# Reordering the start of a diffusion transformer block: silu first, matvecs ahead of transposes, two engines sharing the PSUM copies, a third transpose buffer

## The chip, the cores and the metric

The kernel runs on one core of one Trainium2 chip. The metric is the device time of one execution in microseconds (us), lower is better. The engines are named as the profile names them: PE (TensorE, matmuls), PEld (its weight loads), DVE (VectorE), ACT (ScalarE), POOL (GpSimd), SP (the engine that issues most DMAs here). The span that the profile gives is shorter than the device time: by 1.7 to 1.8 us in the executions of the kernel before.

All ratios are the mean time of one kernel's fast runs over that of the other's fast runs of the same rounds, so they are not quite the ratio of the medians that stand beside them.

## The reference

One block of a diffusion transformer, with B = 2, N = 256 (so 512 rows), D = 1152, two heads and an MLP of width 4608, in bf16:

```python
mod = (silu(c) @ w_mod).reshape(B, 6, 1, D)
shift_a, scale_a, gate_a, shift_m, scale_m, gate_m = [mod[:, i] for i in range(6)]
h = layernorm(x) * (1 + scale_a) + shift_a
q, k, v = split(h @ wqkv)
a = softmax(q @ k.T * Dh ** -0.5) @ v @ wo
x = x + gate_a * a
h2 = layernorm(x) * (1 + scale_m) + shift_m
return x + gate_m * (gelu(h2 @ w_fc1, approximate=True) @ w_fc2)
```

## The kernel before

The part that matters is the head: everything before the first matmul of q and k ("qk"). It needs two things. One is LayerNorm 1 of x, transposed (`lnT`). The other is the modulation: silu(c), transposed (`sT`), times the first six 384-column chunks of `w_mod` (54 small matmuls, called matvecs here). A chunk of weights is 128 x 9 x 384 bf16, 864 KB, in rows of 768 bytes. Each chunk's result is copied from PSUM, turned by three 128x2 matmuls into `modT`, and then `lnT` is multiplied and shifted into `hT`, which the qk matmuls read.

```python
ps_tr = ctx.enter_context(tc.tile_pool(name="ps_tr", bufs=2, space=PSUM))   # transposes
# silu(c): one exp on ACT, three small operations on DVE
nc.scalar.activation(out=c_e, in_=cT_ps, func=ACT.Exp, scale=-1.0)
nc.vector.tensor_scalar(...); nc.vector.reciprocal(...)
nc.vector.tensor_tensor(out=sT[:, :, 0:B], ...)
# ... in mod_mm_multi: 9 matvecs per chunk, then
    nc.vector.tensor_copy(out=m_sb, in_=ps[:, 0:CW])          # always DVE
# LayerNorm 1: statistics and normalisation of all four tiles on DVE
for t in range(TT):
    layernorm_tile(x_sb[:, t, :], ln, False)
for k in range(KD):                                            # 36 transposes
    for t in range(TT):
        nc.tensor.transpose(out=pt[:, t, :], in_=ln1[t][:, k*P:(k+1)*P], identity=ident)
    # copy to lnT, alternately by DVE and ACT
for g in range(NC3):                                           # three pairs of chunks
    m0 = mod_mm(g); m1 = mod_mm(NC3 + g)
    mod_fin_T(m0, g, 0, False); mod_fin_T(m1, NC3 + g, 1, True)
    # six modulations into hT, dealt out to DVE, ACT and POOL
# ... (cut) then qk_chunk(0, split=True): its weights in three column thirds, rows of 256 bytes
```

The source order is a priority for the scheduler, not the order on the engines. Each engine runs its own queue in order.

## Time and profile before

| Quantity | Before |
|---|---|
| Device time, median of 4 runs (lowest, highest) | 265.78 us (265.41, 266.69) |
| The execution that was profiled | 266.69 us, span 264.9 us |
| PE busy | 242.8 us, 92% of the span |
| First matvec; first qk matmul; second group of 9 qk matmuls | 16.43; 26.36; 28.62 us |
| Sixth chunk of `w_mod` landed; its matvecs start | 23.17; 24.38 us |

First, lines of the profile's page for the kernel before: busy time by engine, then busy tenths in 40 equal slices of 6.6 us each, and the granted clock of the array.

```profile
span 264.9 us, 3724 instructions
PE 242.8 (92%) x1556; PEld 135.4 (51%) x1567; DVE 79.7 (30%) x227; ACT 65.0 (25%) x138; POOL 16.8 (6%) x29
PE   0068999999999999998999999999999999999994
PEclk9999999999999999999999999999999999999999
```

PE is full from the fifth slice on, except for a dip at LayerNorm 2. So, apart from the tail in the last slice, time can only be won in the first four slices and in that dip. The clock row says full speed everywhere.

The timeline of PE in the kernel before: start, duration, line, operation, how many, and the idle time ahead with what ended it.

```profile
16.11 0.40 PE L259 MATMUL tr_ps<-ident,ln 128*128 128x128 bf16 x2 [1.26 <-DVE ln L222]
16.43 1.78 PE L135 MATMUL mod_ps<-wchunk,sT 128*32 128x384 bf16 x14
...
19.84 1.03 PE L259 MATMUL tr_ps<-ident,ln 128*128 128x128 bf16 x8
...
24.38 0.66 PE L135 MATMUL mod_ps<-wchunk,sT 128*32 128x384 bf16 x9
25.23 0.23 PE L158 MATMUL modT_ps<-sel4T,m_sb 128*128 128x2 bf16 x3 [0.20 <-DVE m_sb L147]
26.29 0.21 PE L158 MATMUL modT_ps<-sel4T,m_sb 128*128 128x2 bf16 x3 [0.83 <-DVE modT L163]
```

Fourteen matvecs take 1.78 us at 16.43 (127 ns each), nine take 0.66 us at 24.38 (73 ns each): the array is slow at first. PE runs the sixth chunk's matvecs at 24.38, 1.2 us after their weights landed, because it is late with the work ahead of them.

The chain of waits behind it in the kernel before, start and length in us:

```profile
24.22 0.42 DVE lnT L262
...
24.71 0.06 DVE m_sb L147
...
25.70 0.47 DVE m_sb L147
26.16 0.08 DVE modT L163
...
26.29 0.21 PE modT_ps L158 x3
26.50 2.07 PE qk_ps L308 x9
28.57 0.05 issue
28.62 1.46 PE qk_ps L308 x6
```

After the matvecs, the copies wait on DVE for their turn, and the qk matmuls wait for those.

Last, windows of the kernel before: from:to, length, then busy time of each engine (instructions), granted clock, DMA share, GB/s.

```profile
16.40:21.40 5.00, 5.00 (x42) 2.03 (x41) 2.62 (x8) 1.07 (x2) 0.55 (x1) 1.00 1.10 326
21.40:26.30 4.90, 3.83 (x60) 2.32 (x60) 4.53 (x15) 3.24 (x7) 2.24 (x4) 1.00 1.26 222
26.40:44.00 17.60, 17.49 (x82) 7.75 (x82) 3.53 (x7) 3.44 (x6) 1.27 (x2) 1.00 1.09 329
```

Once the qk matmuls run, PE leaves 0.1 us of 17.6 unused, so a head that ends earlier by some amount shortens the kernel by about that amount.

### The profile page before, as it was taken

What the parts mean: (1) busy time and instruction counts of PE and PEld (TensorE: products, weight loads), DVE (VectorE), ACT (ScalarE), POOL (GpSimd) and SP (SyncE); (2) the same over time, 40 slices, a digit from 0 to 9 for tenths busy, and PEclk for the clock granted to TensorE, in tenths of its full rate; (3) what the DMA queues carried; (4) which work ended last, traced back from release to release, by engine and by line L of the source; (5) the groups of instructions that cost most, each with busy time, mean ns of one, the idle gap of its engine ahead of it and who ended that gap; (6) DMA issues with size and microseconds to landing.
All of it is one profiled execution on the core that took longest, in us unless ns stands there. A gap on an engine that the chain in (4) does not pass through costs nothing.

```text
span 264.9 us, 3724 instructions
## 1 busy us (share of the span) xinstructions
PE 242.8 (92%) x1556; PEld 135.4 (51%) x1567; DVE 79.7 (30%) x227; ACT 65.0 (25%) x138; POOL 16.8 (6%) x29
## 2 busy tenths in 40 slices
PE   0068999999999999998999999999999999999994
PEld 0025444455565666567844444444466656666562
DVE  0877313445453746882100000000011111122111
ACT  2005210223312532687532332323300000000000
POOL 2113100022102000100000000000000000000000
PEclk9999999999999999999999999999999999999999
DMA  6999999999999998057265555544440193000000
GB/s 211 356 326 246 335 327 326 327 327 326 326 327 326 326 327 265 1 160 243 57 212 139 153 177 181 156 134 136 135 132 30 26 325 97 17 15 15 27 20 15
DMA packets 67755, 50.37 MB, mean 190 GB/s; under 512 B 4635, under 2 KB 67227, under 8 KB 67739
## 3 DMA queue, kind: packets, MB, share of 16 engines
q1 hardware_dynamic: 67136, 48.96, 63.0%
q10 hardware_dynamic: 603, 1.18, 1.2%
q8 instruction: 12, 0.20, 0.3%
q14 instruction: 4, 0.03, 0.0%
HBM read 48.96 MB, written 1.18 MB: 189 GB/s over the span
## 4 chain that ended last, share of the span: by engine, by line
PE 85%; DVE 5%; issue 3%; DMA 3%; ACT 2%; POOL 1%; ACTq 0%; POOLq 0%
PE f_ps L476 27%; PE f_ps L465 22%; PE qk_ps L308 13%; PE v_ps L322 7%; PE wo_ps L414 4%; PE mod_ps L135 4%; DMA x_sb<-in_x_dram 3%; PE f1h_ps L458 2%; PE o_ps L364 2%; PE s_ps L336 2%; DVE ln_stats L211 1%; PE tr_ps L259 1%; ACT ln L435 1%; PE gate_ps L169 1%; PE tr_ps L229 1%
## 5 line engine op out<-in xcount | busy, mean ns | idle before, releaser
L476 PE MATMUL f_ps<-wchunk,gT 128*128 128x384 bf16 x432 | 70.4, 326 | 0.0
L465 PE MATMUL f_ps<-h2T,wchunk 128*128 128x512 bf16 x264 | 58.1, 379 | 0.3
L476 PEld LDWEIGHTS <-gT 128*128 128x128 bf16 x432 | 42.3, 98 | 28.0
L484 DVE TENSOR_TENSOR f_tmp<-f_ps,gate_bc 128x384 f32<-128x384 f32 x12 | 6.7, 558 | 120.1 <-PE f_ps L476 120.1
L465 PEld LDWEIGHTS <-wchunk 128*128 128x128 bf16 x270 | 26.4, 98 | 31.6
L308 PE MATMUL qk_ps<-hT,wchunk 128*128 128x512 bf16 x157 | 35.5, 379 | 0.3
L466 ACT ACTIVATE gT<-f_ps 128x512 bf16<-128x512 f32 x30 | 17.9, 597 | 40.6 <-PE f_ps L465 39.2
L308 PEld LDWEIGHTS <-wchunk 128*128 128x128 bf16 x162 | 15.7, 98 | 18.7 <-issue 0.5
L414 PE MATMUL wo_ps<-wchunk,aT 128*128 128x384 bf16 x108 | 18.7, 326 | 0.0
L322 PE MATMUL v_ps<-wchunk,hT 128*128 128x384 bf16 x108 | 18.0, 326 | 0.0
L259 PE MATMUL tr_ps<-ident,ln 128*128 128x128 bf16 x36 | 4.3, 258 | 11.9 <-DVE ln L222 11.9
L322 PEld LDWEIGHTS <-hT 128*128 128x128 bf16 x108 | 10.6, 98 | 6.7
L414 PEld LDWEIGHTS <-aT 128*128 128x128 bf16 x108 | 10.3, 98 | 6.0
L458 PE MATMUL f1h_ps<-h2T,wchunk 128*128 128x256 bf16 x108 | 13.1, 272 | 0.0
L135 PE MATMUL mod_ps<-wchunk,sT 128*32 128x384 bf16 x162 | 11.7, 360 | 0.0
L458 PEld LDWEIGHTS <-wchunk 128*128 128x128 bf16 x108 | 10.3, 98 | 1.4 <-issue 0.2
L347 POOL TENSOR_SCALAR pn<-p_sb,rinv 128x256 bf16<-128x256 bf16 x8 | 7.3, 924 | 46.1 <-DVE rinv L345 46.1
L147 DVE CAST m_sb<-mod_ps 128x384 bf16<-128x384 f32 x18 | 9.4, 551 | 2.7 <-PE mod_ps L135 2.5
L259 PEld LDWEIGHTS <-ln 128*128 128x128 bf16 x36 | 2.4, 110 | 14.7 <-DVE ln L222 13.1
L211 DVE BATCH_NORM_STATS2 ln_stats<-x_sb 128x6 f32<-128x384 bf16 x12 | 6.0, 536 | 6.3 <-DMA x_sb<-in_x_dram 6.3
L422 ACT ACTIVATE sq_junk<-x 128x384 bf16<-128x384 f32 x12 | 6.2, 515 | 5.9 <-DVE x L418 4.3
L417 DVE TENSOR_TENSOR wo_tmp<-wo_ps,gate_bc 128x384 f32<-128x384 f32 x12 | 6.7, 555 | 2.2 <-PE wo_ps L414 2.2
(79 smaller groups left out, 155.6 us busy)
## 6 DMA issues: line engine op xcount, KB each, us to landing
wchunk<-in_w_fc_dram SPq DMA_DIRECT2D x24, 864.0 KB, 5.4
wchunk<-in_w_mod_dram SPq DMA_DIRECT2D x18, 864.0 KB, 10.2
wchunk<-in_wqkv_dram SPq DMA_DIRECT2D x8, 864.0 KB, 10.1
wchunk<-in_wo_dram SPq DMA_DIRECT2D x3, 864.0 KB, 10.1
x_sb<-in_x_dram ACTq DMA_DIRECT2D x4, 288.0 KB, 7.3
out_dram<-o_sb SPq DMA_DIRECT2D x12, 96.0 KB, 1.6
wchunk<-in_wqkv_dram SPq DMA_DIRECT2D x3, 288.0 KB, 7.6
c<-in_c_dram ACTq DMA_DIRECT2D x1, 4.5 KB
```

The costliest lines, as they stand in the source:

```text
L135: nc.tensor.matmul(ps[32 * g : 32 * (g + 1), 0:CW], lhsT=sT[:, k, :], rhs=wt[:, k, :], start=(g not in gs[:k]), stop=(g not in gs[k + 1 :] ...
L147: nc.vector.tensor_copy(out=m_sb, in_=ps[:, 0:CW])
L211: nc.vector.bn_stats(out=stats[:, i, :], in_=src[:, i * CW : (i + 1) * CW])
L259: nc.tensor.transpose(out=pt[:, t, :], in_=ln1[t][:, k * P : (k + 1) * P], identity=ident)
L308: nc.tensor.matmul(ps, lhsT=wt[:, k, i * P : (i + 1) * P], rhs=hT[:, k, :], start=(k == 0), stop=(k == KD - 1))
L322: nc.tensor.matmul(ps[:, 0:CW], lhsT=hT[:, k, t * P : (t + 1) * P], rhs=wt[:, k, :], start=(k == 0), stop=(k == KD - 1))
L347: nc.gpsimd.tensor_scalar(out=pn, in0=p_sb, scalar1=rinv[:, 0:1], scalar2=None, op0=ALU.mult)
L414: nc.tensor.matmul(ps[:, 0:CW], lhsT=aT[:, k, t * P : (t + 1) * P], rhs=wo_t[c3][:, k, :], start=(k == 0), stop=(k == KD - 1))
L458: nc.tensor.matmul(ps[:, 0:N], lhsT=wt[:, k, i * P : (i + 1) * P], rhs=h2T[:, k, b * N : (b + 1) * N], start=(k == 0), stop=(k == KD - 1))
L465: nc.tensor.matmul(ps, lhsT=wt[:, k, i * P : (i + 1) * P], rhs=h2T[:, k, :], start=(k == 0), stop=(k == KD - 1))
L466: nc.scalar.activation(out=gT[:, f, :], in_=ps, func=ACT.Gelu_apprx_tanh)
L476: nc.tensor.matmul(ps[:, 0:CW], lhsT=gT[:, kf, t * P : (t + 1) * P], rhs=wts[kf // KD][:, kf % KD, :], start=(kf == 0), stop=(kf == KF - 1),)
```

## The change

The intent is to let qk start earlier and to speed up the transposes in LayerNorm 2:

- silu(c) goes ahead of the LayerNorm statistics on DVE, and tiles 2 and 3 take their statistics on ACT;
- matvecs of the first chunks go ahead of the transposes on PE;
- the copies of the modulation alternate between DVE and ACT;
- four dummy matmuls stand in a wait for the last chunks;
- the transposes get three PSUM buffers in place of two.

The diff, cut to its core:

```diff
-    ps_tr = ctx.enter_context(tc.tile_pool(name="ps_tr", bufs=2, ...))
+    ps_tr = ctx.enter_context(tc.tile_pool(name="ps_tr", bufs=3, ...))
...
+    def warm(n, after):
+        wp = ps_tr.tile([P, 512], FP32, name="warm_ps", tag="tr")
+        for _ in range(n):
+            w = nc.tensor.matmul(wp, lhsT=ident, rhs=x_sb[:, 0, 0:512], start=True, stop=True)
+            order_after(w, after, "keep PE busy")
...
-            nc.vector.tensor_copy(out=m_sb, in_=ps[:, 0:CW])
+            if mod_evac_i[0] % 2 == 0:
+                cp = nc.vector.tensor_copy(out=m_sb, in_=ps[:, 0:CW])
+            else:
+                cp = nc.scalar.copy(out=m_sb, in_=ps[:, 0:CW])
...
+    def layernorm_tile_act(src, dst):
+        nc.scalar.activation(out=dst, in_=src, func=ACT.Identity, accum_out=s12[:, 0:1])
+        nc.scalar.activation(out=dst, in_=src, func=ACT.Square, accum_out=s12[:, 1:2])
+        ...
-    for g in range(NC3):
-        m0 = mod_mm(g)
-        m1 = mod_mm(NC3 + g)
-        ...
+    for t in (2, 0, 3, 1):
+        ln1_tile(t)
+    m_of[0] = mod_mm(0)
+    m_of[3] = mod_mm(3)
+    m_of[1] = mod_mm(1)
+    ln1_transposes(2, after=last_mod_mm[0])
+    ln1_transposes(0)
+    m_of[4] = mod_mm(4)
+    ln1_transposes(3, after=last_mod_mm[0])
+    ln1_transposes(1)
+    fin_pair(0)
+    modulate_group(0)
+    fin_pair(1)
+    m_of[2] = mod_mm(2)
+    first_after[0] = warm(4, last_mod_mm[0])
+    m_of[5] = mod_mm(5)
+    fin2 = mod_fin_T(m_of[2], 2, 0, False)
+    modulate_group(1, last_copy[0], fin2)
+    mod_fin_T(m_of[5], 5, 1, True)
+    modulate_group(2)
```

## The prediction

> **What bounds the kernel now.** TensorE. The engine table gives PE 242.8 of 264.9 us, and the slices show PE nearly full from the fifth slice to the end. In the windows view PE is busy 17.5 of 17.6 us (26.4 to 44) and 55.6 of 56 (44 to 100). So this change can only pay where PE still waits: before the first qk matmul at 26.36, and while LayerNorm 2 is transposed (123.9 to 128.3: PE busy 3.6 of 4.4 us).
>
> **The head now.** In the timeline the modulation matvecs start at 16.43, because silu(c) waits on VectorE behind the LN1 statistics (ready 16.13). They and 36 transposes keep PE full from 16.4 to 21.4, slowly: 14 matvecs took 1.78 us (127 ns each) at 16.4, 18 took 0.99 us (55 ns) at 44. The Trainium skill, "TensorE: Matmul & The Clock Gate", Part 1, says that an idle array runs at half clock until it has been busy for about 3.4 us; these spacings agree, though the page's clock row shows full clock throughout. The sixth matvec chunk runs at 24.38 to 25.04, although (issue plus time to landing) it landed at 12.9 + 10.3 = 23.2. A chain follows: PSUM copies on VectorE (the second ends 26.16), 128x2 matmuls, modT, modulations to 28.14. The ninth qk matmul waits for that; the second qk group starts at 28.62.
>
> **What the change does.** silu(c) comes before most LN1 work (tiles 2 and 3 take their statistics on ScalarE): matvecs should start near 14.4. Matvecs go ahead of transposes, evacuations alternate between VectorE and ScalarE, four dummy matmuls fill a wait, transposes get a third PSUM buffer. It adds about 1 us of PE dummies where PE would wait for the DMA, and about 5 us of ScalarE, idle there now.
>
> **On the critical path.** PE is no longer late for the sixth chunk, but cannot pass its landing, 23.2, nor the first third of the qk weights, 15.6 + 8.9 = 24.5; DMA moves 326 GB/s without a gap from 7 us on, and its order is not changed. From 23.2: matvecs 0.8, copy on ScalarE 0.5, matmuls and modT 0.5; but ScalarE then still has four modulations (1.1 us a pair), ending near 26.6. First qk matmul 24.7, second group 26.9: gain 1.7 us. It can hardly exceed 2: the second qk chunk lands only at 30.7, and PE will want it at 30.8.
>
> Third PSUM buffer: VectorE copies take 0.41, ScalarE 0.56 us; with two buffers each slot also waits for its transposes. The last modulation comes some 1 us earlier, but the new order puts fewer MLP matmuls between the transposes (about 10 for 17 before), so 0.3 to 0.5 us net. Filler copies on ScalarE: about 0.
>
> Sum: 2.1 us, all of it by an earlier start, not by less PE work.
>
> **Predicted: 263.6 us, between 262.3 and 265.2 (8 in 10). Faster by over 2%: 0.04; within 2%: 0.95; slower by over 2%: 0.01.**
>
> **What would show it.** Right: first matvec at 14 to 15 us, first qk matmul at 24.5 to 25, second group near 27, everything until 110 us moved by the same 1.5 to 2 us; the DMA landings unmoved; PE busy time up by about 1 us. LN2: last transposes evacuated about 1 us sooner relative to LN2's last normalisation, MLP matmuls ending 0.3 us sooner relative to it. Wrong: qk start at 26 (PE still cold and late, or ScalarE late), or a PE wait for the second qk chunk.
>
> **What would make it wrong.** Gaps while waiting for chunks could keep the array at half clock into the qk matmuls (up to 1.7 us lost). ScalarE runs its two 1152-element passes on tile 2 before exp(c); were x late, silu would be too. If the landings move, the gain moves with them.

## The result

| | Before | After |
|---|---|---|
| Median of the runs of these rounds | 265.69 us (16 runs, 265.41 to 266.84) | 265.14 us (11 runs, 264.89 to 265.34) |
| Ratio, 95% interval | | 0.9967 [0.9953, 0.9981] |
| Profiled execution, span | 266.69, 264.9 us | 264.94, 263.0 us |

Within 2%. By the medians the change gains 0.55 us, by the ratio 0.9 us (0.0033 of 266), by the two profiled executions 1.75 us (1.9 us in their spans). That these three differ is the whole story. All outputs are right.

The profile after agrees with the prediction nearly line by line. The page of the kernel after:

```profile
span 263.0 us, 3744 instructions
PE 242.4 (92%) x1560; PEld 135.7 (52%) x1571; DVE 74.0 (28%) x215; ACT 73.9 (28%) x157; POOL 17.7 (7%) x29
PEclk9999999999999999999999999999999999999999
```

The timeline of PE in the kernel after:

```profile
13.34 2.95 PE L155 MATMUL mod_ps<-wchunk,sT 128*32 128x384 bf16 x27 [9.86 <-DVE sT L115]
16.23 0.68 PE L318 MATMUL tr_ps<-ident,ln 128*128 128x128 bf16 x9
...
23.14 0.32 PE L155 MATMUL mod_ps<-wchunk,sT 128*32 128x384 bf16 x1
...
24.65 0.23 PE L186 MATMUL modT_ps<-sel4T,m_sb 128*128 128x2 bf16 x3 [0.43 <-ACT m_sb L173]
24.74 5.50 PE L404 MATMUL qk_ps<-hT,wchunk 128*128 128x512 bf16 x24
```

The chain of waits in the kernel after:

```profile
12.84 10.26 DMA wchunk<-in_w_mod_dram
...
23.14 0.32 PE mod_ps L155
...
24.11 0.49 ACT m_sb L173
...
24.65 0.23 PE modT_ps L186 x3
24.88 5.15 PE qk_ps L404 x23
```

The chain of the head now begins with the sixth chunk's DMA, which lands at 23.10. PE takes it 0.04 us later, ACT copies at once, and qk starts at 24.74 (predicted 24.7; 26.36 before). The second group starts at 26.84 (predicted 26.9; 28.62 before).

LayerNorm 2 in the kernel before, from the last normalisation to the next MLP matmuls:

```profile
122.85 1.35 ACT L435 ACTIVATE ln<-x,ln_nbias,ln_rstd 128x1152 bf16<-128x1152 f32 x1 [1.09 <-DVE ln_nbias L433]
127.70 4.90 PE L458 MATMUL f1h_ps<-h2T,wchunk 128*128 128x256 bf16 x42
```

The same in the kernel after:

```profile
121.26 1.35 ACT L531 ACTIVATE ln<-x,ln_nbias,ln_rstd 128x1152 bf16<-128x1152 f32 x1 [1.09 <-DVE ln_nbias L529]
125.18 5.52 PE L554 MATMUL f1h_ps<-h2T,wchunk 128*128 128x256 bf16 x48
```

From the end of the last normalisation to the end of these matmuls it was 124.20 to 132.60, 8.4 us, and is 122.61 to 130.70, 8.1 us: 0.3 less, as predicted. The last copy of the transposes ends 3.19 us after the normalisation where it ended 4.12 us after it, 0.9 us sooner, also as predicted. So head and LayerNorm 2 give 1.8 + 0.3 = 2.1 us between these two profiles. The stretch between them is 0.2 us longer than before (95.8 us from the second qk group to the end of the normalisation, 95.6 before), which leaves 1.9 us in the span, and the time outside the span takes nearly another 0.2. The question is why the median moved by a quarter of that.

### The profile page after: what moved, and what is told of

Its sections match the earlier page's. It is cut to its first block, busy times and chain, and to the rows that moved or that the text cites. A ratio compares the mean times of both kernels' runs of the same rounds, so it can differ in the third digit from the quotient of the medians.

```text
span 263.0 us, 3744 instructions
## 1 busy us (share of the span) xinstructions
PE 242.4 (92%) x1560; PEld 135.7 (52%) x1571; DVE 74.0 (28%) x215; ACT 73.9 (28%) x157; POOL 17.7 (7%) x29
## 4 chain that ended last, share of the span: by engine, by line
PE 84%; SPq 5%; DMA 4%; issue 2%; DVE 2%; ACT 2%; POOL 1%; POOLq 0%
PE f_ps L572 27%; PE f_ps L561 22%; PE qk_ps L404 13%; PE v_ps L418 7%; SPq L66 5%; PE wo_ps L510 4%; DMA wchunk<-in_w_mod_dram 4%; PE mod_ps L155 2%; PE f1h_ps L554 2%; PE o_ps L460 2%; PE s_ps L432 2%; ACT ln L531 1%; PE gate_ps L197 1%; PE tr_ps L265 1%; POOL ln_rstd L527 1%
## 5 line engine op out<-in xcount | busy, mean ns | idle before, releaser
L510 PEld LDWEIGHTS <-aT 128*128 128x128 bf16 x108 | 10.3, 98 | 6.2
L155 PEld LDWEIGHTS <-sT 128*32 128x32 bf16 x162 | 4.7, 101 | 15.9 <-DVE sT L115 10.0
L173 ACT CAST m_sb<-mod_ps 128x384 bf16<-128x384 f32 x9 | 4.3, 481 | 12.4 <-PE mod_ps L155 12.4
L582 DVE TENSOR_TENSOR o_sb<-f_tmp,x 128x384 bf16<-128x384 f32 x12 | 6.7, 559 | 0.4
L514 DVE SCALAR_TENSOR_TENSOR x<-wo_tmp,x_sb 128x384 f32<-128x384 f32 x12 | 6.7, 557 | 0.2
```

Source lines behind the costliest of these rows:

```text
L155: last_mod_mm[0] = nc.tensor.matmul(ps[32 * g : 32 * (g + 1), 0:CW], lhsT=sT[:, k, :], rhs=wt[:, k, :], start=(g not in gs[:k]), stop=(g n ...
L510: nc.tensor.matmul(ps[:, 0:CW], lhsT=aT[:, k, t * P : (t + 1) * P], rhs=wo_t[c3][:, k, :], start=(k == 0), stop=(k == KD - 1))
L514: nc.vector.scalar_tensor_tensor(out=x1[:, t, cs], in0=tmp, scalar=1.0, in1=x_sb[:, t, cs], op0=ALU.mult, op1=ALU.add, accum_out=sums[:, 0 ...
```

## The experiments

Two theories stood against each other. In the expectations they may be spoken of as A and B.

- **Theory A: the baseline.** The profiled execution of the kernel before was one in which the array reached full clock late. In its faster executions it gets there earlier, PE is not late for the sixth chunk, and the change has little left to gain. The change does not make the head much faster; it makes it independent of when the clock rises.
- **Theory B: the landings, or profiling.** The DMA landings differ from run to run or the profiler slows one kernel more, and the 1.9 us between the profiles is not real.

The trace records the granted clock as intervals, and this shows what the page's row hides. The record of the kernel before begins at 21.43 us with "full speed"; ahead of that there is no record, and the page's row prints full. In the kernel after, the record begins at 16.06 us. The lengths of the recorded intervals of full clock are multiples of 3.413 us (242.346 is 71 of them, 245.76 is 72, and the dip in one run below is 3.413 itself). The Trainium skill, "TensorE: Matmul & The Clock Gate", Part 1 ("What's actually happening"), says that the array starts at half clock and is released by activity in a window of 3413 ns that runs freely.

### The unchanged kernel again, profiled six times

No edit. These were run to see whether other executions of the kernel before look different.

> The kernel before, unchanged, to see another of its executions. Theory A (the profile I predicted from was one of the slow executions of the kernel before, 266.69 us of 265.4 to 266.8, in which the array came to full clock only at 21.4 us): most of these runs lie at 265.4 to 265.7; a profile of such a run has a span near 263.7 us, its second qk group starts near 27.5 us and not at 28.6, and the matvecs lie about 55 ns apart well before 21 us. Theory B (profiling itself, or the landing of the DMAs, moves the head): profiles always have a span near 264.9 us and the second qk group at 28.6, or the sixth matvec chunk lands about 1 us earlier in the faster executions.

> A second look at the kernel before, to have one more execution of it. Theory A: the span is either near 263.7 us or near 264.9 us, and the array reaches the full clock earlier in the first case; DMA landings are the same within 0.3 us. Theory B: 264.9 us.

> The kernel before once more, for the trace of one of its faster executions (mean clock 1.0, span 263.6 to 264.0, near half of its runs so far). Theory A: if this one is such an execution, the array is at full clock (matvecs 55 ns apart) by 19 us, the sixth chunk's matvecs start within 0.5 us of their landing at 23.1, the second qk group starts at 27.3 to 27.7. Theory B: the landings are earlier instead. A slow execution (span 264.7) says nothing new.

> The kernel before once more, one more draw for the trace of a faster execution; the theories expect of it what they expect of the third look (A: full clock by 19 us and the second qk group at 27.3 to 27.7; B: earlier landings).

> The kernel before, another draw for the trace of a faster execution (span 263.6 to 264.0). Theory A: full clock by 20 us, the sixth chunk's matvecs within 0.8 us of their landing at 23.1, second qk group at 27.3 to 27.7. Theory B: earlier landings, full clock at 21.4 as before. A span near 264.8 says nothing new.

> The kernel before, another draw for the trace of a faster execution; the same is expected of it as of b_again5: by theory A full clock by 20 us and the second qk group at 27.3 to 27.7, by theory B earlier landings.

The first, timed in 5 rounds, took 266.11 us (265.68 to 266.57, ratio 1.0008 [0.9991, 1.0026]). In order of the time at which the clock record begins, with the two profiles of the prediction:

```
execution     full clock from   sixth chunk lands   second qk group   span     time
b_again5      19.25             22.96               27.24             263.7    265.52
b_again6      19.31             23.14               27.32             263.8    265.59
before        21.43             23.17               28.62             264.9    266.69
b_again       21.51             23.03               28.41             264.7    266.46
b_again2      21.71             23.15               28.55             264.8    266.60
b_again4      21.72             23.02               28.46             264.7    266.54
b_again3      22.55             23.03               29.14             265.4    267.18
after         16.06             23.10               26.84             263.0    264.94
```

The landing of the sixth chunk is the same within 0.2 us in all of them, and does not go with the time. The start of full clock does: from 19.3 to 22.55 us, the second group moves from 27.24 to 29.14 and the time from 265.52 to 267.18. The first matvec moves too, from 15.98 to 16.54 us, as the last tile of x lands between 10.28 and 10.98 us, but this does not order the times: it starts at 16.10 in b_again2 and at 16.43 in before, and their second groups start at 28.55 and 28.62. The first five profiles of the unchanged kernel (counting that of the prediction) all fell in the late kind; that is put down to chance, and nothing here shows it to be more.

The executions that were timed and not profiled can be placed roughly as well. In the profiles of the kernel before, the only half clock on record comes at the very end of the program, after the last full window, so the mean clock of an execution tells where its windows lie. Of the 34 executions of before that stand beside the later runs, with their mean clocks, the nine fastest (265.41 to 265.78 us) all have 1.000. Of the next seven (265.88 to 266.10) six have .997, of the next ten (266.29 to 266.51) eight have .998, and of the eight slowest (from 266.59) seven have .999. As an estimate from span and mean clock, the clock was full from about 20.3 us at .997 and from about 22 us at .999. So the time goes with the phase in these too, with four exceptions.

Two of them compare cleanly, as their first matvecs start 0.08 us apart. The timeline of PE in the late one (b_again):

```profile
16.06 1.78 PE L135 MATMUL mod_ps<-wchunk,sT 128*32 128x384 bf16 x14
...
19.47 1.03 PE L259 MATMUL tr_ps<-ident,ln 128*128 128x128 bf16 x8
20.44 0.83 PE L135 MATMUL mod_ps<-wchunk,sT 128*32 128x384 bf16 x5
...
24.18 0.66 PE L135 MATMUL mod_ps<-wchunk,sT 128*32 128x384 bf16 x9
```

And in the early one (b_again5):

```profile
15.98 1.78 PE L135 MATMUL mod_ps<-wchunk,sT 128*32 128x384 bf16 x14
...
19.36 0.62 PE L259 MATMUL tr_ps<-ident,ln 128*128 128x128 bf16 x8
19.91 0.51 PE L135 MATMUL mod_ps<-wchunk,sT 128*32 128x384 bf16 x5
...
23.21 0.66 PE L135 MATMUL mod_ps<-wchunk,sT 128*32 128x384 bf16 x9
```

The same program, the same instructions: up to 19 us they run alike, then eight transposes take 1.03 us in one and 0.62 us in the other, and the sixth chunk's matvecs end up at 24.18 or 23.21. In the second, PE starts them 0.25 us after the weights land (22.96). The lateness on which the prediction built is not there. The second group then starts at 27.24, and the kernel after, at 26.84, gains 0.4 us in the head and 0.3 in LayerNorm 2: 0.7, which is the difference of the spans (263.7 and 263.0). Of the 0.4 us only 0.1 lies ahead of the sixth chunk's matvecs (23.21 and 23.14); the rest lies in the shorter chain of copies behind them. In device time such executions lose less than 0.7 us to the kernel after, as this has 0.2 us more outside the span: the nine early ones in the rounds of the result average 265.55 us, those of the kernel after 265.10. Theory B falls: the landings agree, and the faster executions of before, profiled, have the faster time. Theory A stands.

### Forcing the clock: dummy matmuls ahead of the head

```diff
+    NWARM = 45
+    wp = ps_tr.tile([P, 512], FP32, name="warm_ps", tag="tr")
+    for _ in range(NWARM):
+        w = nc.tensor.matmul(wp, lhsT=ident, rhs=kT4m[:, 0, :], start=True, stop=True)
...       # (cut) one after another, and the first LayerNorm transpose behind the last of them
```

> The kernel before, with 45 dummy matmuls (128x512) from 3.5 us to about 15 or 16 us, where the array idles, so that the clock is full when the matvecs start. Theory A: the slow executions vanish, all runs within 0.3 us of 265.4 to 265.6; the sixth chunk's matvecs start at its landing, near 23.2 us, and the second qk group near 27.5. Theory B: still both kinds of runs, 265.4 to 266.8, as for the kernel before.

It took 266.93 us (266.64 to 267.48), ratio 1.0039 [1.0022, 1.0056]: slower, and a failed test. The clock was up at 7.66 us but did not stay up. Windows of this kernel (columns as above, the granted clock is third from the end):

```profile
14.49:17.90 3.41, 1.46 (x16) 0.68 (x13) 2.35 (x8) 0.14 (x1) 1.00 (x2) 1.00 1.10 326
17.90:21.31 3.41, 3.41 (x24) 1.37 (x19) 1.24 (x4) 1.03 (x2) 0.00 (x0) 0.50 1.10 326
```

And the clock row of its page, where the half clock does show, since it comes after the first record:

```profile
PEclk9988999999999999999999999999999999999999
```

The dummies ended near 15.0 us, PE was busy for 1.46 of the next 3.41 us, and for the following 3.41 us, with the real work, the clock was halved. The longest single gap in the first of these windows was 1.43 us. More transposes also came ahead of the matvecs, which began only at 17.65 us. So this run says nothing about theory A, and it does not tell how much of the loss is the clock's and how much the order's.

### One part alone: third transpose buffer

```diff
-    ps_tr = ctx.enter_context(tc.tile_pool(name="ps_tr", bufs=2, ...))
+    ps_tr = ctx.enter_context(tc.tile_pool(name="ps_tr", bufs=3, ...))
```

> The kernel before with the third transpose buffer in PSUM alone. The prediction's account of the LN2 stretch: 0.3 us (0.2 to 0.5) shorter between the end of LN2's last normalisation and the end of the 256-column MLP matmuls; in time 0.2 to 0.4 us less than before. If the buffer is worth nothing on its own, the ratio is 1.000.

It took 265.96 us (265.70 to 266.74), ratio 1.0006 [0.9986, 1.0026]. Its LayerNorm 2 stretch is 8.1 us, the predicted 0.3 less. The gain can't be seen in the time: the clock's phase moves the time of an execution by 1 us and more, and none of its six runs fell in the early kind, while about half of the runs of before beside them did.

### One part alone: silu first

```diff
-            nc.vector.bn_stats(out=stats[:, i, :], ...)
+            bn = nc.vector.bn_stats(out=stats[:, i, :], ...)
+            # only the first one: ordered behind the last operation of silu(c)
```

> The kernel before with one order dependency: silu(c) on VectorE ahead of the LN1 statistics, nothing else. Theory A (the spread of the kernel before, 265.4 to 266.6, is how late PE is for the sixth modulation chunk while the array is still at half clock): matvecs start as soon as their chunks land, from 6.5 us on; the sixth chunk's run at 23.1 to 23.4 in every execution; the second qk group starts at 27.3 to 27.7; runs within 0.4 us of each other near 265.4, whatever the clock's phase. Rival C (what the change gains is the shorter chain behind the sixth chunk, not the earlier start): no gain, 265.4 to 266.6 as before. A risk for both: matvecs spread out over the landings keep the array cold into the qk matmuls, then it is slower than before.

It took 269.62 us (269.18 to 270.11), ratio 1.0131 [1.0113, 1.0149]: 3.6 us slower than the 266.04 of the kernel before in the same rounds. The timeline of PE tells why:

```profile
9.70 1.14 PE L135 MATMUL mod_ps<-wchunk,sT 128*32 128x384 bf16 x9 [7.31 <-DVE sT L115]
12.27 1.12 PE L135 MATMUL mod_ps<-wchunk,sT 128*32 128x384 bf16 x9 [1.42 <-DMA wchunk<-in_w_mod_dram]
...
23.17 0.82 PE L135 MATMUL mod_ps<-wchunk,sT 128*32 128x384 bf16 x5 [1.64 <-DMA wchunk<-in_w_mod_dram]
...
27.91 1.06 PE L267 MATMUL tr_ps<-ident,ln 128*128 128x128 bf16 x8
```

The matvecs start at 9.70, far earlier than in either kernel, and then each chunk's matvecs wait for their DMA with idle time in between. The transposes stand behind them in the queue: the last 20 of the 36 run from 26.09 us on, among the first qk matmuls. The Trainium skill, "TensorE: Matmul & The Clock Gate", Part 2 ("Step-by-step: what each phase is for"), says that matmuls stay in program order, and this trace agrees: transposes whose data was there waited behind matvecs whose data was not. The clock record begins only at 30.15 us. Theory A had expected a time near 265.4 us here; that was missed, and the risk named beside it came true. So by itself the early silu is a loss; the change brings an explicit order of matvecs and transposes along with it.

### One part alone: copies on two engines

```diff
-            nc.vector.tensor_copy(out=m_sb, in_=ps[:, 0:CW])
+            if mod_evac_i[0] % 2 == 0:
+                nc.vector.tensor_copy(out=m_sb, in_=ps[:, 0:CW])
+            else:
+                nc.scalar.copy(out=m_sb, in_=ps[:, 0:CW])
+            mod_evac_i[0] += 1
```

> The kernel before with the modulation copies alternating between VectorE and ScalarE, nothing else. Theory A: little, PE is late for the sixth chunk all the same; the chain behind it gets up to 0.5 us shorter at best; spread with the clock's phase as before, about 1 us. Rival C: the better part of the gain of the change, mean 0.5 us or more below the kernel before and little spread.

It took 265.95 us (265.30 to 266.58), ratio 0.9994 [0.9977, 1.0011]. In its profile the second group starts at 28.09 us with full clock from 20.83, which lies between the early and the late executions of before. By itself it is worth nothing that this spread would let one see.

### The change with two transpose buffers

```diff
-    ps_tr = ctx.enter_context(tc.tile_pool(name="ps_tr", bufs=3, ...))
+    ps_tr = ctx.enter_context(tc.tile_pool(name="ps_tr", bufs=2, ...))
```

> The changed kernel with the transposes' PSUM pool back at two buffers. If the third buffer is worth what the traces of b_tr3 show in the LN2 stretch (0.3 us), it takes 265.4 instead of 265.1; more only if the head needs it too (its transposes and dummies share the pool), then the second qk group starts later than 26.9.

It took 265.93 us (265.67 to 267.65), ratio 1.0002 [0.998, 1.0023]: without the third buffer no gain over the kernel before is left that these runs could show. LayerNorm 2 is back at 8.4 us, and the second group starts at 27.58 in place of 26.84. In its timeline the transposes wait for copies (0.23, 0.24 and 0.16 us) and the last of them run at 23.32, so the sixth chunk's matvecs come at 24.51 and not at 23.14. Most of that delay is the dummies: they keep their place ahead of these matvecs and now run at 23.55, when the sixth chunk has already landed (23.10), for nearly 1 us. The clock was up later than in the profile of the change (18.20 us), but the next run had 18.70 and still reached 26.83 (with a landing 0.2 us earlier), so the late second group is put down to the buffer together with the fixed place of the dummies. The prediction had counted the buffer for LayerNorm 2 alone; in this order the head's gain needs it too.

### The change without the dummy matmuls

```diff
-    first_after[0] = warm(4, last_mod_mm[0])
```

> The changed kernel without its four dummy matmuls. They fill a wait of about 1 us for the sixth chunk, and the traces so far show the clock falling only after a stretch of some 3.4 us with little work (b_prewarm). So: no difference, 265.0 to 265.3. If the dummies are what holds the clock up into the qk matmuls, some runs are 1 us or more slower.

It took 265.58 us (264.82 to 267.62), ratio 0.9992 [0.9962, 1.0022]. No difference had been expected, and that was wrong. Three of its six runs (264.82 to 265.14) equal the change, which was timed in other rounds, at a mean granted clock of 1.000; the other three had .992, .992 and .987 and took 266.01, 266.07 and 267.62. As an estimate, .992 is 4.2 us of half clock, one dip of 3.413 us and the end of the program. In the profiled run, one of the first kind, there is a wait of 0.87 us for the sixth chunk where the dummies stood. That the clock falls there in the slower runs is read from the mean clock alone, since no slow run was profiled. With the dummies none of the eleven runs has a mean clock below .997, and their spread is 0.45 us, where this has 2.8.

### Beyond the change: earlier qk work, longer rows, a warm array

The change's chain starts at a DMA, so four further versions looked for time there. The last is the best kernel found. Their diffs are against the kernel after or the version before, and are shortened. The first loads the first third of the qk weights by contraction rows (rows of 768 bytes, not of 256) ahead of the sixth modulation chunk and runs three qk groups side by side, beginning with the parts of `hT` that are ready:

```diff
+    def load_w0(kk):
+        nc.sync.dma_start(out=w0[:, 3*kk : 3*kk+3, :], in_=wqkv_v[:, 3*kk : 3*kk+3, 0:CW])
+    load_w0(0)
+    wm5 = load_w(wmod_v, 0, 5 * CW)
+    load_w0(1)
+    load_w0(2)
...
+    qk0(0, 0); qk0(0, 1)              # k = 0..2 of groups 0 and 1
+    m_of[5] = mod_mm(5, wm5)          # then the sixth chunk's matvecs
+    qk0(0, 2); qk0(1, 0)
```

> A version after the changed kernel, against the DMA wall in the head: the first qk weights come in thirds of k (768-byte rows, not 256), the first of them before the sixth modulation chunk; the first three qk groups run side by side, k 0 to 2 of all, then the sixth chunk's matvecs, then k 3 to 5, then k 6 to 8; groups 0 and 1 of the modulation are finished before the sixth chunk lands. Worked out from the changed kernel's trace: the three groups end at 29.3 to 29.6 us instead of 30.7, the second qk chunk lands near 28.5; 263.7 to 264.2 us, 1 to 1.4 below the changed kernel. If the wait for the sixth chunk only moves (chain behind it not covered by 18 qk matmuls), 264.6 to 265.0.

It took 263.96 us (263.73 to 264.09), ratio 0.9917 [0.9903, 0.9931]. The first qk matmul runs at 22.71 us, before the sixth chunk has landed.

The second loads the first four modulation chunks in pairs, so that rows are 1536 bytes:

```diff
+    def load_pair(j, at):
+        nc.sync.dma_start(out=wt, in_=wmod_v[:, 0:KD, j * CW : (j + 2) * CW])
-    m_of[0] = mod_mm(0)
+    wm0, wm1 = load_pair(0, 0); wm3, wm4 = load_pair(3, 1)
+    m_of[0] = mod_mm(0, wm0)
```

> a_best3, with the first four modulation chunks loaded in pairs of adjacent chunks, so that a descriptor row is 1536 bytes and not 768 (into the memory that the MLP's hidden activations use later). The DMA moved 363 GB/s in the 5 us where the 2304-byte rows of x were in, 326 GB/s with 768-byte rows alone. If the row length sets the rate, the sixth chunk lands 0.4 to 1 us earlier and the kernel takes 263.2 to 263.6 us; if not, 263.9 to 264.1 as a_best3, or later, as the first matvecs then wait for a pair.

It took 264.08 us (263.13 to 264.40), ratio 0.9917 [0.9902, 0.9933]. The sixth chunk landed at 21.75 us, 2.1 us earlier than in the first version (23.88), where 0.4 to 1 had been expected. Between 11 and 14 us, with only the weight queue moving, the DMA ran at 388 GB/s with these rows and at 344 GB/s in the first version; in both, once only 768-byte rows remain, it is 326. The Trainium skill, "DMA: Bandwidth & Descriptors" ("Why small descriptors are slow"), names a fixed cost of about 3 bus cycles for each packet beside one cycle for 32 bytes, and 32 bytes of descriptors for each operation. An estimate from the first would be 27 cycles for 24 useful ones at 768 bytes and 51 for 48 at 1536, a gain of 6%, or 8% with the descriptors counted as one more cycle; the measured one is 13 to 19% (388 over 344 and over 326). The edit also makes each of these DMAs twice as large, so the row length is not the only difference. The time did not follow: the sixth chunk's matvecs now start 2.2 us after the chunk lands (23.99), behind other work of PE. A spread of 1.3 us is back; that this is the clock's phase is not tested here.

The third put the sixth chunk's matvecs back ahead of qk and finished the first modulation pair earlier:

```diff
     ln1_transposes(0)
+    fin_pair(0)
...
+    first_after[0] = warm(2, last_mod_mm[0])
+    m_of[5] = mod_mm(5, wm5)
     modulate_group(1)
...
-    qk0(0, 0); qk0(0, 1); m_of[5] = mod_mm(5, wm5); qk0(0, 2); qk0(1, 0)
+    for i in range(3): qk0(0, i)
```

> a_best4 retuned: the sixth chunk lands at 21.7 us with the longer rows, so its matvecs now come before the qk matmuls, the first modulation pair is finished before the transposes of later tiles, two dummies instead of four. The first qk matmul should start near 21.9 (22.6 in a_best4) and the three qk groups end near 28.5 (29.2): 263.2 to 263.6 us in its faster executions. The head is bound by TensorE from 14 us on, so by theory A the runs spread by 1 us or so with the clock's phase, as those of a_best4 did (263.1 to 264.4).

It took 264.41 us (263.82 to 264.68), ratio 0.9917 [0.9895, 0.994]. The expectation was missed: qk started at 23.97 us, 2 us later than expected. The array was still at half clock until 17.66 us and the first matvecs were slow (18 in 2.10 us), and the sixth chunk's started at 23.37 us, 1.6 us after it had landed (21.79). That the one follows from the other is what the next version tests.

The fourth is the third with 34 dummy matmuls from 3 us on, in the time in which PE has nothing to do:

```diff
+    NWARM = 34
+    wp0 = ps_mm.tile([P, 512], FP32, name="warm0_ps", tag="mm")
+    for _ in range(NWARM):
+        w = nc.tensor.matmul(wp0, lhsT=ident, rhs=kT4m[:, 0, :], start=True, stop=True)
...       # (cut) one after another, and the first matvec behind the last of them
```

> a_best5 with 34 dummy matmuls from 3 us to about 13 us, where the array idles, and work without a gap after them. Theory A: full clock from the first matvec in every execution, all runs within 0.4 us, as fast as the fastest of a_best5 or faster (262.6 to 263.2). If the phase of the clock is not what spreads the runs, the spread stays; if the clock falls again as in b_prewarm, they are slower.

It took 262.68 us (262.44 to 263.21), ratio 0.9863 [0.9836, 0.989], the best and 1.7 us below the third version of the same rounds (1.4 us by the ratios), by dummies alone. The sixth chunk's matvecs now start at 21.89 us, 0.1 us after its landing, and qk at 22.49. Here is what the failed dummy test should have been. The timeline of PE:

```profile
3.05 9.87 PE L143 MATMUL warm_ps<-kT4m,ident 128*128 128x512 bf16 x34
13.93 1.15 PE L164 MATMUL mod_ps<-gT,sT 128*32 128x384 bf16 x18 [1.00 <-DVE sT L115]
...
22.49 2.12 PE L410 MATMUL qk_ps<-hT,wchunk 128*128 128x512 bf16 x9
```

One of its windows, in which the clock stayed up though PE was not full:

```profile
14.70:18.11 3.41, 2.33 (x34) 1.18 (x29) 2.68 (x9) 1.26 (x4) 0.55 (x1) 1.00 1.10 350
```

The clock record of this run begins at 7.88 us, with full clock from there to 0.2 us before the end of the program. Eighteen matvecs take 1.15 us where the third version needed 2.10. So the cold array costs this head, which is bound by PE, 1.4 to 1.7 us, measured by the edit itself. The expected spread of 0.4 us was missed (0.77): two of the five runs have a mean clock of .993 and are 0.6 us slower than the rest, so the clock may still fall in some.

## Why the prediction was right or wrong

**The head, 1.7 us: right for the profile it was read from.** First matvec 13.34 (predicted near 14.4, between 14 and 15; even earlier), first qk matmul 24.74 (24.7), second group 26.84 (26.9), landings unmoved (23.17 and 23.10).

**LayerNorm 2, 0.3 us of a range of 0.3 to 0.5: right,** in the change and in the third buffer alone (8.4 to 8.1 us both times).

**PE busy time up by 1 us: wrong,** 242.8 to 242.4. The dummies did run (three in the head's window, 1.0 us), but at full clock the 36 transposes of the head take 2.9 us in place of 4.3.

**The sum, "2.1 us", taken from 265.78: here it failed.** The 2.1 us is the difference to the profiled execution, and that took 266.69 us. 266.69 minus 2.1 is 264.6; the profiled execution after took 264.94. The prediction took the gain from the median instead, as though the median execution had the same head. The false step, as the prediction put it, is "The sixth matvec chunk runs at 24.38 to 25.04, although ... it landed at 12.9 + 10.3 = 23.2", read as a property of the kernel. It is a property of the executions with a late clock. In those with an early clock (19.3 us) the matvecs run at 23.21 to 23.87, the term "gain 1.7 us" measures 0.4 us, and the whole gain is 0.7 us in the span and about 0.45 us in the time. Of the 16 runs of before in the rounds of the result, nine lie at 265.74 or below and five at 266.54 or above; the mean gain of 0.9 us is the mixture. Two smaller terms were missing from the sum, 0.2 us more between the head and LayerNorm 2 and 0.2 us more outside the span. That 265.14 us still lies within the stated range, by 0.06 us, is owed to its width and does not support the sum.

**What the prediction knew and did not use.** It cited the half clock and saw that the page's row hides it. The Trainium skill, "TensorE: Matmul & The Clock Gate", Part 1, also says that the phase varies from run to run and that the ramp costs under 1% of a span. Both hold here: the profiled executions of before differ by 1.7 us with it, 0.6% of 266. But the effect that was to be predicted is 0.8%, so a term of that size could not be left out. Four timed runs that ranged over 1.3 us, with the profiled one the slowest, were the warning, and they were in the material.

**What stays open.** What activity in a window raises or keeps the clock is not settled (the numbers are in the last section). The phase of the runs that were timed but not profiled is inferred from their times and mean clocks. In the kernel before the clock itself was never moved by an edit, as the one attempt failed; that it makes the lateness rests there on executions of the same program, and on an edit only in the last version. Why the kernel after has 0.2 us more outside its span is not known.

## What to carry to other kernels

Before subtracting a gain from a median, look at which execution the profile shows: compare its own time with the others, and take the gain from that one. A stage that follows a mostly idle array can be late because of the clock alone, and by an amount that differs from run to run; then a reordering buys mainly steadiness, and dummy matmuls in idle time can buy the time itself, if the clock does not fall again before the work begins. Starting one producer earlier was a loss here (3.6 us) where its consumer's queue then waited in order for data, so early starts and queue order have to be changed together.

## What the Trainium skill lacked or had wrong

- "TensorE: Matmul & The Clock Gate", "HAM oscillation": it gives "no PE-idle gaps >~3.4µs" as the rule for staying at full clock. Here the clock was halved after a window of 3.41 us with 1.46 us of PE work, in which the longest gap was 1.43 us (b_prewarm). It stayed up after two windows with 1.49 us of work and 1.9 us idle at their end (a_nodummy from 257.63 us, a_best4 from 256.14 us). So the length of a gap does not decide in these runs. From cold it rose after windows with 2.71 us of work (after, from 12.65 us) and 2.97 us (a_tr2, from 14.78 us), and did not after 2.93 us (b_again3, from 15.72 us) and 3.21 us (b_silu, from 23.32 us). So the busy time that the profile counts does not decide the rise either; what does is not settled.
- The same page, Part 1: "the ramp penalty is <1% of a typical kernel span" fits here (1.7 us between profiles, 0.6%), but it does not say that this can exceed the gain in question: the executions of the kernel before range from 265.41 to 267.51 us over all rounds, and the change gains 0.9 us.
- No page says that a clock row made from the trace's records shows full clock ahead of the first record. It did here up to 21.43 us, with 14 matvecs taking 127 ns each on average, where 18 at full clock take 55.
- "DMA: Bandwidth & Descriptors", "Why small descriptors are slow": the overheads named there give an estimate of 6 to 8% between rows of 768 and of 1536 bytes; the runs show 326 to 344 against 388 GB/s. The line of its "Specifications" that full rate needs at least 512 bytes does not tell of this step above 512.
